# K^T by one crossbar transpose a head instead of 16 TensorE transposes, in a one-core attention forward and backward kernel

## Chip, cores and metric

The kernel runs on one core of a Trainium2 chip. The metric is the device time of one execution in microseconds (us); lower is better. Executions of one kernel differ by some 0.2 to 0.6%, so what matters here is timed in several rounds, in turn with the kernel before on the same chip.

## The reference

One layer, forward and backward, in bf16. S = 2048 rows, D = 576, H = 32 heads of 128, F = 4608:

```python
def _A_ref(x, k_cache, v_cache, wq, wo):
    q = (x @ wq).reshape(B, Sq, H, Dh).transpose(0, 2, 1, 3)
    scores = jnp.einsum("bhqd,bhkd->bhqk", q, k_cache) * (Dh ** -0.5)
    p = _softmax(scores, axis=-1)
    o = jnp.einsum("bhqk,bhkd->bhqd", p, v_cache)
    return o.transpose(0, 2, 1, 3).reshape(B, Sq, H * Dh) @ wo
# ... _B_ref: a gated MLP
xn = _layernorm(x);  s = _A_ref(xn, ...);  g = _silu(_B_ref(xn, ...))
return x + s * g
# the outputs: this, and its gradients by x, k_cache, v_cache, wq, wo, w_gate, w_up, w_down
```

## The kernel before

Each head takes two phases of 16 slots, one slot for each block of 128 query rows. In a slot of phase 1 TensorE (PE) makes 128 x 2048 scores from Q^T and K^T, ScalarE (ACT) makes their exponentials into a slab `Pq`, and the SP queue turns the slab with the DMA crossbar into `PT`, which PE reads five slots later (`skew` is 5). Phase 2 does the same for the gradients: `dp` on PE, `Pq` rewritten by ACT and VectorE (DVE), turned into `dST`, read five slots later. So 32 crossbar transposes of 512 KB a head run on one queue.

K is loaded as `Kn`, 16 blocks with keys on the partitions. The scores need K^T, in `KT`, half of the tile `KQ`. K^T of head h+1 is made in phase 2 of head h, because phase 1 of head h still reads `KT`:

```python
def prep_kt(hs):
    KTv = hs.KT[:].rearrange("p (t q) -> p t q", q=P)
    pe_transpose_blocks(lambda j: hs.Kn[:, j, :], 0, NT, lambda g, n: KTv[:, g:g + n, :], "s")

def transpose_slab(hs, qt, name):                      # PT and dST
    T = wpt.tile([P, NT, P], bf, name=name, tag="PT")
    nc.sync.dma_start_transpose(T[:], hs.slabs[qt][:])
    return T

def plan(h):
    # ...
    pl = b2 - 2 * NT if h else None                    # the first slot of phase 2 of head h - 1
    if h:
        for c in range(4):
            put(pl + q(c), 0, lambda c=c: load_k(hd(), c, 4))
            put(pl + q(skew + 3 + c), 0, lambda c=c: load_v(hd(), c, 4))
        # ...
        put(pl + q(skew + 3), NT * P, lambda: prep_kt(hd()))
    # ...
    for qt in range(NT):
        put(b2 + qt + skew, NT * P // 2, lambda qt=qt: tail2(hd(), qt, 0))   # reads dST of qt
        put(b2 + qt + skew, NT * P // 2, lambda qt=qt: tail2(hd(), qt, 1))
```

A scheduler orders each engine's instructions when the program is built, and may issue an instruction well before the slot in which the text has it. It moves the V loads, written in slots 8 to 11, to 9 to 15 us after the start of phase 2 (slots 3 and 4), and the K loads into phase 1.

## Time and profile before

| | before |
|---|---|
| time, first three runs | 5043.2 us (5036.47 to 5043.98) |
| attention, 32 heads | about 490 to 3650 us |
| one head, PE-bound: phase 1 + phase 2 | 49.56 + 48.13 us |

The page of the profile: busy time of an engine and its share of the span, then the share that the chain of waits gives each engine.

```profile
PE 4922.4 (97%) x53584; PEld 3474.9 (69%) x54480; DVE 2581.2 (51%) x6705; ACT 2574.1 (51%) x4636; POOL 950.4 (19%) x1481
...
PE 89%; issue 4%; DMA 3%; DVE 2%; ACT 1%; POOL 0%; SPq 0%; POOLq 0%; ACTq 0%; DVEq 0%
```

PE's own instructions are the limit. What the 16 transposes of a head cost there is read from the timeline of PE in head 4 (start, length, what). A group's length holds the latency of its last matmul, so cost is the distance between starts:

```profile
946.23 0.38 PE L698 MATMUL dp<-VT,dOT 128*128 128x512 bf16 x1
946.66 1.06 PE L146 MATMUL acct<-ident,Kn 128*128 128x128 bf16 x16
947.56 0.59 PE L698 MATMUL dp<-VT,dOT 128*128 128x512 bf16 x2
```

From 946.66 to 947.56 is 0.90 us: 56 ns a transpose. Two groups of the page's kind, the copies that leave PSUM and the reads of `dST` (after the first bar busy us and mean ns; after the second the engine's idle time before them and what ended it):

```profile
L40 ACT COPY KQ<-acct 128x1024 bf16<-128x1024 bf16 x62 | 59.7, 1015 | 15.8 <-PE acct L146 15.8
...
L675 PE MATMUL acc<-Kn,dST 128*128 128x128 bf16 x8192 | 551.3, 219 | 10.1 <-DMA dST<-Pq 6.5
```

The SP queue has two views that seem to disagree. Its waits in head 4 (870 to 972 us; us in total, times, longest):

```profile
SPq L622 <- ACT Pq L646: 32.8, 15, 4.7
SPq L622 <- DVE Pq L701: 15.2, 9, 3.7
SPq L622 <- DVE Pq L706: 14.4, 6, 3.4
SPq L622 <- DVE junk L687: 4.4, 2, 2.8
SPq L622 <- ACT o_n L48: 2.3, 1, 2.3
```

Together 69 us of 102. Its timeline from 900 to 972 us, in which neighbours are merged and the first group begins before the window:

```profile
894.76 31.29 SPq L622 DMA_TRANSPOSE PT<-Pq  x11
926.76 47.78 SPq L622 DMA_TRANSPOSE dST<-Pq  x16
```

### The profile page before, as it was taken

What the parts mean: (1) busy time and instruction counts of PE and PEld (TensorE: products, weight loads), DVE (VectorE), ACT (ScalarE), POOL (GpSimd) and SP (SyncE); (2) the same over time, 40 slices, a digit from 0 to 9 for tenths busy, and PEclk for the clock granted to TensorE, in tenths of its full rate; (3) what the DMA queues carried; (4) which work ended last, traced back from release to release, by engine and by line L of the source; (5) the groups of instructions that cost most, each with busy time, mean ns of one, the idle gap of its engine ahead of it and who ended that gap; (6) DMA issues with size and microseconds to landing.
All of it is one profiled execution on the core that took longest, in us unless ns stands there. A gap on an engine that the chain in (4) does not pass through costs nothing.

```text
span 5053.4 us, 128161 instructions
## 1 busy us (share of the span) xinstructions
PE 4922.4 (97%) x53584; PEld 3474.9 (69%) x54480; DVE 2581.2 (51%) x6705; ACT 2574.1 (51%) x4636; POOL 950.4 (19%) x1481
## 2 busy tenths in 40 slices
PE   8999999999999999999999999999789999999999
PEld 3445777777777787777778777777646666555554
DVE  4544666666566666666656666665425444200111
ACT  4432766666666676666667666666313333211000
POOL 3322111111111111111111111111122222211000
PEclk9999999999999999999999999999999999999999
DMA  7886999999999999999999999999996665797976
GB/s 249 271 202 171 212 208 211 203 211 209 207 214 214 201 212 207 210 205 211 214 202 209 215 206 207 208 213 202 197 201 204 193 183 181 213 266 187 173 141 121
DMA packets 2762675, 1031.39 MB, mean 204 GB/s; under 512 B 2665249, under 2 KB 2669474, under 8 KB 2762082
## 3 DMA queue, kind: packets, MB, share of 16 engines
q1 hardware_dynamic: 2659746, 699.38, 75.0%
q0 software_dynamic: 101728, 323.05, 20.1%
q8 instruction: 428, 7.01, 0.6%
q14 instruction: 165, 1.35, 0.1%
q10 hardware_dynamic: 608, 0.59, 0.0%
HBM read 175.31 MB, written 182.13 MB: 71 GB/s over the span
## 4 chain that ended last, share of the span: by engine, by line
PE 89%; issue 4%; DMA 3%; DVE 2%; ACT 1%; POOL 0%; SPq 0%; POOLq 0%; ACTq 0%; DVEq 0%
PE acc L734 17%; PE acc L675 17%; PE acc L960 13%; PE sp L628 7%; PE acc L1131 7%; PE dp L698 7%; PE acc L213 6%; PE g_ps L446 3%; PE u_ps L448 3%; PE dh L1013 3%; PE acc L531 2%; PE acct L146 2%; PE acc L930 2%; DMA dST<-Pq 1%; DVE Pq L701 1%
## 5 line engine op out<-in xcount | busy, mean ns | idle before, releaser
L646 ACT ACTIVATE Pq<-sp 128x1024 bf16<-128x1024 f32 x1024 | 1047.1, 1023 | 330.4 <-PE sp L628 199.1
L734 PEld LDWEIGHTS <-Pq 128*128 128x128 bf16 x16384 | 1002.9, 98 | 240.5 <-issue 1.1
L705 ACT ACTIVATE t<-dp,negdelta 128x1024 bf16<-128x1024 f32 x512 | 571.1, 1116 | 222.6 <-PE dp L698 169.0
L701 DVE SCALAR_TENSOR_TENSOR Pq<-dp,negdelta,Pq 128x1024 bf16<-128x1024 f32 x512 | 654.9, 1279 | 38.6 <-PE acc L675 37.5
L675 PEld LDWEIGHTS <-PT 128*128 128x128 bf16 x8192 | 503.3, 98 | 142.2 <-DMA PT<-Pq 20.9
L675 PE MATMUL acc<-Vn,PT 128*128 128x128 bf16 x8192 | 548.4, 219 | 26.6 <-DMA PT<-Pq 19.6
L675 PE MATMUL acc<-Kn,dST 128*128 128x128 bf16 x8192 | 551.3, 219 | 10.1 <-DMA dST<-Pq 6.5
L734 PE MATMUL acc<-dOn,Pq 128*128 128x128 bf16 x8192 | 547.4, 219 | 10.2 <-DVE junk L687 0.2
L628 PE MATMUL sp<-KQ 128*128 128x512 bf16 x1762 | 548.4, 380 | 2.6 <-ACT Pq L646 2.4
L698 PE MATMUL dp<-VT,dOT 128*128 128x512 bf16 x1728 | 540.0, 379 | 7.6 <-DVE Pq L701 7.6
L734 PE MATMUL acc<-Qn,Pq 128*128 128x128 bf16 x8192 | 540.6, 219 | 3.4
L706 DVE TENSOR_TENSOR Pq<-t,Pq 128x1024 bf16<-128x1024 bf16 x512 | 354.3, 692 | 365.8 <-ACT t L705 359.0
L675 PEld LDWEIGHTS <-dST 128*128 128x128 bf16 x8192 | 492.0, 98 | 69.5 <-DMA dST<-Pq 8.6
L715 ACT ACTIVATE dq_n<-acc,rsc 128x128 bf16<-128x128 f32 x512 | 188.1, 367 | 333.0 <-PE acc L675 331.9
L1147 DVE SCALAR_TENSOR_TENSOR junk<-acc,xn_all 128x512 f32<-128x512 f32 (+1 forms) x32 | 13.9, 453 | 637.0 <-ACT dxn L1146 637.0
L748 POOL DMA_DIRECT2D out_dram<-kvo x256 | 140.2, 548 | 1019.0 <-DVE kvo L746 1011.0
L669 POOL DMA_DIRECT2D on_d<-o_n x128 | 97.0, 758 | 750.7 <-DVE junk L687 396.7
L1015 DVE TENSOR_TENSOR du_blk<-dh,ah 128x256 bf16<-128x256 f32 x288 | 120.1, 417 | 191.6 <-PE dh L1013 189.5
L50 DVE TENSOR_SCALAR o_n<-acc,rinv_all 128x128 bf16<-128x128 f32 x352 | 123.2, 350 | 180.9 <-PE acc L675 180.9
L1146 ACT ACTIVATE dxn<-acc 128x512 f32<-128x512 f32 (+1 forms) x32 | 12.8, 406 | 393.6 <-PE acc L1131 386.2
L633 DVE TENSOR_REDUCE rs_all<-rsp 128x1 f32<-128x2 f32 x512 | 78.0, 152 | 256.3 <-ACT Pq L646 254.1
L646 ACT ACTIVATION_READ_ACCUMULATOR Pq<-sp 128x1 f32 x1024 | 200.4, 196 | 0.0
(206 smaller groups left out, 6949.9 us busy)
## 6 DMA issues: line engine op xcount, KB each, us to landing
out_dram<-kvo POOLq DMA_DIRECT2D x256, 128.0 KB, 4.2
ah<-a_d POOLq DMA_DIRECT2D x18, 1024.0 KB, 7.1
ah<-h_d POOLq DMA_DIRECT2D x18, 1024.0 KB, 9.5
du_d<-du_blk POOLq DMA_DIRECT2D x18, 1024.0 KB, 8.1
dg_d<-dg_blk POOLq DMA_DIRECT2D x18, 1024.0 KB, 9.9
h_d<-h_row POOLq DMA_DIRECT2D x64, 256.0 KB, 3.5
a_d<-a_row POOLq DMA_DIRECT2D x64, 256.0 KB, 3.7
x_all<-in_A_k_cache_dram SPq DMA_DIRECT2D x64, 256.0 KB, 4.0
```

What stands on the lines that cost most here:

```text
L213: nc.tensor.matmul(av[:, :CH], lhsT=w[:, i, :], rhs=srcT[:, i, cs], start=(i == 0), stop=(i == DT - 1))
L628: nc.tensor.matmul(sp[:, c * CH:(c + 1) * CH], lhsT=hs.QT[:, qt * P:(qt + 1) * P], rhs=hs.KT[:, hf * HW_ + c * CH: hf * HW_ + (c + 1) * CH ...
L646: nc.scalar.activation(Pq[:, hsl], sp[:], AF.Exp, scale=SCALE, accum_out=hs.rsp[:, hf:hf + 1])
L675: nc.tensor.matmul(hs.acc[:, 0, :], lhsT=T[:, kt, :], rhs=rhs[:, kt, :], start=(kt == 0), stop=(kt == NT - 1))
L698: nc.tensor.matmul(dp[:, c * CH:(c + 1) * CH], lhsT=hs.dOT[:, qt * P:(qt + 1) * P], rhs=hs.VT[:, hf * HW_ + c * CH: hf * HW_ + (c + 1) * C ...
L701: nc.vector.scalar_tensor_tensor(Pq[:, hsl], dp[:], hs.negdelta[:, qt:qt + 1], Pq[:, hsl], op0=ALU.add, op1=ALU.mult)
L705: nc.scalar.activation(t[:], dp[:], AF.Identity, bias=hs.negdelta[:, qt:qt + 1], scale=1.0)
L706: nc.vector.tensor_tensor(Pq[:, hsl], t[:], Pq[:, hsl], op=ALU.mult)
L715: nc.scalar.activation(hs.dq_n[:, qt % G4, :], hs.acc[:, 0, :], AF.Copy, scale=hs.rsc[:, qt:qt + 1])
L734: nc.tensor.matmul(self.tile[:, j, :], lhsT=self.slabs[qt][:, kt * P:(kt + 1) * P], rhs=self.rhs[:, qt, :], start=(qt == self.lo), stop=(q ...
L960: nc.tensor.matmul(accs[j][:, :nn], lhsT=lhs[:, st, cols], rhs=rhs[:, st, n0:n0 + nn], start=(st == 0), stop=(st == NT - 1))
L1131: nc.tensor.matmul(self.accs[sl][j][:, :nn], lhsT=ch[:, kk, sl * P:(sl + 1) * P], rhs=wT[:, k0 + kk, n0:n0 + nn], start=(self.k + kk == 0) ...
```

## The change

The intent is to take work from PE, the limit, and give it to the DMA crossbar, which does 32 such transposes a head already. K^T of head 0 is still made on PE, before attention.

```diff
+            def turn_nat(dst, src):
+                nc.sync.dma_start_transpose(dst[:].rearrange("p (t q) -> p t q", q=P), src[:].rearrange("p t d -> p (t d)"))
+
             def start_head(h):
...
-                    put(pl + q(skew + 3), NT * P, lambda: prep_kt(hd()))
+                    put(pl + q(skew + 3), 0, lambda: turn_nat(hd().KT, hd().Kn))
```

In the built program the scheduler does not leave the new transpose in slot 8. It puts it between the 15th and the 16th `PT` of the previous head, where its wait, for the last score matmul that reads `KT`, ends. The orders of ACT, DVE and POOL differ by ACT's removed copies alone, that of PE by the removed transposes and one `dp` pair a head moved within its slot.

## The prediction

> **What bounds the kernel.** The page gives PE 97% busy, the chain of waits 89% PE. Attention (486 to 3590 us, 32 heads, 97.0 us each) has PE busy 3040 of 3104 us in the stretch table, DVE 63%, ACT 68%. The timeline of a middle head (874 to 971 us) is back-to-back matmuls with one PE wait of 0.24 us. In all of attention the wait list gives PE 18.2 us for PT transposes (15.4 of it once, in the last head) and 2.3 us for dST. So PE instruction time is the limit; DMA, at 9 in the page's slices, is nearly hidden.
>
> **What changes.** Removed for 31 heads: 16 PE transposes and two ACT copies of 1.015 us. In the timeline the 16 transposes start at 946.66 and the next matmul at 947.56: 0.90 us, 56 ns each, like any 128-column matmul. (The Trainium skill, "TensorE: Matmul & The Clock Gate", Part 4, gives about 275 ns for one; here 219 ns is the latency, hidden by the pipeline. At 275 ns 4.4 us a head, 2.7%, would be saved; I do not believe it.) PE saves 31 x 0.89 = 27.6 us, 0.55%. The copies are off the path: PE never waits for them.
>
> Added: a 512 KB crossbar transpose a head on the SP queue, 33 instead of 32. The instruction order shows it between the previous head's 15th and 16th PT, waiting for PE (the last score matmul that reads K^T) and four Kn loads. POOL, DVE and ACT orders are otherwise unchanged; on PE one dp pair moves within its slot. Kn landed by about 900 us in that head, the scores end at 922, K^T is needed at 971: 40 us of slack, and no blocking on loads.
>
> **Cost of the addition.** SP waits for compute 69 of 97 us, so issuing has room. Transposes land in 3.6 to 3.9 us uncontended, in 8 to 9 beside the Kn and Vn loads, and recover 1 to 2 us per 2.65 us slot, so one occupies about 2 us (estimate; 512 KB at the 261 GB/s of the skill's "DMA: Bandwidth & Descriptors", "DMA_TRANSPOSE effective BW", is also 2.0). It delays the last PT and the first one or two dST by about 2 us, where landing is 3.7 to 5.5. A dST is issued at 926.76 and read at 937.82, so 11 us are there. Tight are the dST beside the Vn loads (landing 9.0, slack 2), 12 us later: the backlog should be gone. I allow 3 us in all for new waits.
>
> **Prediction.** 5043.2 - 27.6 + 3: about 5019 us (ratio 0.995), range 5008 to 5034. Faster by over 2%: 0.01; within 2%: 0.97; slower: 0.02.
>
> **What would show it.** The head period falls from 97.0 to 96.1 us, the difference all in attention. PE busy falls by about 27 us. The matmuls acct<-Kn fall from 496 to 0, the ACT copies KQ<-acct from 62 to 0. KQ<-Kn appears as 31 DMA transposes landing in 4 to 7 us. PE waits for PT and dST stay under 30 us. DMA bytes rise by 16 MB.
>
> **What would make it wrong.** The new transpose blocks its queue (Kn late in other heads, or its wait on PE is for a later instruction than the last score matmul): every PT and dST behind it is late, several us a head, over 100 us. Or DMA is nearer saturation than landing times suggest, and dST waits appear in each head. Or DVE, 94% busy early in the second phase, paces the shortened slot, so less than 0.89 us a head is won.

## More of the kernel before

PE waited for `dST` only 6.5 us in the whole run.

Last, how loaded the DMA engines are around the start of phase 2 in head 20 (at 2487.0 us), by stretch: length, busy time of PE, PEld, DVE, ACT and POOL (with counts), granted clock, DMA share, GB/s. The share adds up packet times over 16 engines and can pass 1, as it does here.

```profile
2479.00:2487.00 8.00, 7.90 (x113) 6.77 (x114) 4.63 (x23) 6.29 (x12) 0.00 (x0) 1.00 1.15 216
2487.00:2491.00 4.00, 3.71 (x50) 2.93 (x48) 3.52 (x11) 2.96 (x6) 0.75 (x1) 1.00 0.82 197
2491.00:2499.00 8.00, 7.89 (x107) 6.56 (x109) 6.84 (x13) 3.77 (x6) 0.88 (x2) 1.00 0.84 190
2499.00:2507.00 8.00, 7.89 (x110) 6.60 (x110) 7.12 (x10) 4.38 (x7) 3.67 (x7) 1.00 1.11 213
```

For the first 12 us of phase 2 the engines have less to do (0.82, 0.84); then the V loads come (POOL, last row) and they are full again. Head 20 shows this more strongly than most: as means over heads 1 to 30 the four stretches have 1.19, 1.13, 1.02 and 1.13, so what there is of quiet lies 4 to 12 us into the phase.

## The result, and the profile after

| | before | after |
|---|---|---|
| median of 4 runs | 5043.59 us (5036.47 to 5046.36) | 5046.65 us (5040.28 to 5060.24) |
| ratio, 95% interval | | 1.0012 (0.9987 to 1.0036) |

Ratios here are the mean time of one kernel's runs over the mean of the other's in the same rounds, so they are not quite the ratio of the medians that are quoted. About 5019 us was predicted; the time did not move. The page, then the transposes' tile, groups and PE waits:

```profile
PE 4900.6 (97%) x53089; PEld 3447.6 (68%) x53984; DVE 2585.6 (51%) x6705; ACT 2520.8 (50%) x4574; POOL 950.7 (19%) x1481
...
PE 86%; DMA 7%; issue 4%; DVE 2%; ACT 1%; POOL 0%; SPq 0%; POOLq 0%; ACTq 0%; DVEq 0%
```

```profile
L610 SPq DMA_TRANSPOSE KQ<-Kn x31: 1471/2627/3736, 534.4 to 3473.3; - x31
```

```profile
L678 PE MATMUL acc<-Kn,dST 128*128 128x128 bf16 x8192 | 557.1, 219 | 34.1 <-DMA dST<-Pq 28.9
```

The 496 weight loads (PEld) of the transposes are gone, 54480 to 53984, and DMA's share of the chain rose from 3% to 7%. (PE's busy time is not compared closely: 896 of its matmul records are missing before and 895 after, against the weight loads, and in e_sp10 and e_split none.) PE now waits 28.9 us for `dST` instead of 6.5. The lengths of the phases, taken from the starts of their first weight loads, say it most plainly. Before, phase 2 is 48.13 us in 27 of 31 heads. After, it is 47.24 us in the best heads, 0.89 us less, just as predicted; but in 17 of 31 it is longer by over 0.3 us, up to 51.88 us, and the 31 together exceed 31 x 47.24 by 35.6 us. Phase 1 is 49.56 us in nearly every head of both.

Head 4 has the 51.88 us. Its SP queue, 900 to 975 us:

```profile
899.93 24.04 SPq L625 DMA_TRANSPOSE PT<-Pq  x9
924.15 2.74 SPq L610 DMA_TRANSPOSE KQ<-Kn  x1
926.99 3.24 SPq L625 DMA_TRANSPOSE PT<-Pq  x1
930.31 44.99 SPq L625 DMA_TRANSPOSE dST<-Pq  x16
```

and the PE waits in its phase 2 (idle time and releaser in brackets):

```profile
941.01 1.07 PE L678 MATMUL acc<-Kn,dST 128*128 128x128 bf16 x16 [1.41 <-DMA dST<-Pq]
...
945.83 1.07 PE L678 MATMUL acc<-Kn,dST 128*128 128x128 bf16 x16 [1.55 <-DMA dST<-Pq]
...
951.60 1.07 PE L678 MATMUL acc<-Kn,dST 128*128 128x128 bf16 x16 [1.18 <-DMA dST<-Pq]
```

This phase starts at 921.78 us, 1.03 before that of the kernel before, yet its first `dST` is issued at 930.31 instead of 926.76. Issuing K^T took 2.74 us; the `PT` behind it was held back and, with its own issue slowed to 3.24 us, held back the first `dST`. The DMA engines, as before for head 20 (phase 2 from 2494.7 us):

```profile
2486.70:2494.70 8.00, 7.90 (x113) 6.70 (x114) 4.70 (x23) 6.29 (x13) 0.00 (x0) 1.00 1.20 216
2494.70:2498.70 4.00, 3.72 (x50) 2.95 (x49) 3.50 (x10) 2.96 (x6) 0.75 (x1) 1.00 1.19 268
2498.70:2506.70 8.00, 6.95 (x90) 5.53 (x91) 6.84 (x13) 3.77 (x7) 0.55 (x1) 1.00 1.16 186
2506.70:2514.70 8.00, 7.77 (x106) 6.53 (x109) 6.52 (x10) 3.43 (x6) 3.99 (x7) 1.00 1.16 264
```

The quiet 12 us are gone: 1.19 and 1.16 where it was 0.82 and 0.84. PE loses in the third row (6.95 of 8 us instead of 7.89). Over heads 1 to 30 the step is smaller and still there: in the third stretch 1.19 in the mean instead of 1.02.

The next table is worked out from every transpose's record in the traces, as means over heads 1 to 30. "Idle" is the SP queue's pause before a `dST` (its start less the end of the issue before); "slack" is the time from a `dST`'s landing to its first use on PE; a dash stands where the trace does not tell the landing, and in some kernels it tells it in part of the heads only (26 or 27 of 30 in after and e_novn, 14 to 16 in e_half and e_sp10).

| kernel | idle before dST 0, 1, 2, 3, 4 | slack of dST 0, 1, 2, 3, 4 |
|---|---|---|
| before | 1.32, 0.69, 0.78, 0.69, 0.11 | 6.3, -, 6.2, 2.1, 2.2 |
| after | 0.09, 0.10, 0.14, 0.16, 0.10 | 3.9, 3.9, 2.5, 0.9, 0.9 |
| e_none | 1.34, 0.63, 0.88, 0.70, 0.09 | 6.4, -, 6.1, 1.9, 1.2 |
| e_copy | 0.26, 0.21, 0.46, 0.40, 0.09 | -, -, 5.2, 1.5, 0.9 |
| e_novn | 0.10, 0.10, 0.11, 0.11, 0.10 | 3.9, 4.3, 3.9, 3.0, 3.2 |
| e_half | 0.45, 0.16, 0.52, 0.56, 0.11 | 5.4, 5.8, 5.2, 1.6, 1.1 |
| e_sp10 | 1.33, 0.43, 0.97, 0.71, 0.13 | 6.5, 6.5, 6.3, 2.4, 1.8 |

Before, the queue had 3.5 us of pause before dST 0 to 3 (1.32 + 0.69 + 0.78 + 0.69) and next to none before dST 4 to 10 (0.09 to 0.18); before dST 11 to 15 they are 0.4 to 1.1 us again. After, those in front are used up (0.49 us left): the first dST is issued 6.2 us after the start of phase 2 instead of 4.0, and dST 4 18.5 instead of 15.2. PE waited for dST 2 most (10.9 us) and for dST 3 (9.8). Of dST 4's lost slack the removal alone explains 1.0 us (e_none, 1.2 instead of 2.2). A single profile is not enough for more: the same kernel profiled again showed 13.4 us of such waits in its steady heads (486 to 3480 us) where the first showed 26.1. The time from the start of the last head to the end of the program is between 1515 and 1542 us in the profiled executions, with a mean granted clock between 0.984 and 0.992, though no edit touches that stretch but for an order of the SP queue told of below. So the rest is timed as well.

### The profile page after: what moved, and what is told of

The parts are those of the page before. It is cut to its first block, busy times and chain, and to the rows that moved or that the text cites. A ratio compares the mean times of both kernels' runs of the same rounds, so it can differ in the third digit from the quotient of the medians.

```text
span 5058.4 us, 127199 instructions
## 1 busy us (share of the span) xinstructions
PE 4900.6 (97%) x53089; PEld 3447.6 (68%) x53984; DVE 2585.6 (51%) x6705; ACT 2520.8 (50%) x4574; POOL 950.7 (19%) x1481
## 3 DMA queue, kind: packets, MB, share of 16 engines
q8 instruction: 424, 6.95, 0.6%
## 4 chain that ended last, share of the span: by engine, by line
PE 86%; DMA 7%; issue 4%; DVE 2%; ACT 1%; POOL 0%; SPq 0%; POOLq 0%; ACTq 0%; DVEq 0%
PE acc L737 17%; PE acc L678 16%; PE acc L963 13%; PE sp L631 7%; PE dp L701 6%; PE acc L1134 6%; PE acc L213 6%; DMA dST<-Pq 3%; PE g_ps L446 3%; PE u_ps L448 3%; PE dh L1016 3%; PE acc L531 3%; PE acct L146 2%; PE acc L933 1%; DMA KQ<-on_d 1%
## 5 line engine op out<-in xcount | busy, mean ns | idle before, releaser
L678 PE MATMUL acc<-Kn,dST 128*128 128x128 bf16 x8192 | 557.1, 219 | 34.1 <-DMA dST<-Pq 28.9
```

The lines of the kernel that those rows point to most:

```text
L678: nc.tensor.matmul(hs.acc[:, 0, :], lhsT=T[:, kt, :], rhs=rhs[:, kt, :], start=(kt == 0), stop=(kt == NT - 1))
```

## The experiments

My first theory, T1 in the expectations: the new transpose takes 2.6 us of the transposing queue where the queue has no time to spare, so the dST behind it come late to the place where the V loads slow their landing. Rivals: total DMA load, wherever it stands (T2), or the loss of the 0.9 us by which the PE transposes had put off the use of dST (T3). In six of the ten programs every order but the one named is that of the changed kernel. In the other four (e_sp12, e_sp8, e_sp10, e_split) the SP queue is kept in the order of the text, and this moves two more transposes, once in the program: those of the stage behind attention, `xnT` and `KQ` from `on_d`. The scheduler had put them among the last head's PT, as SP's timeline of e_again shows:

```profile
3542.15 4.84 SPq L582 DMA_TRANSPOSE xnT<-on_d  x1
3547.08 15.85 SPq L625 DMA_TRANSPOSE PT<-Pq  x6
3563.02 5.25 SPq L582 DMA_TRANSPOSE KQ<-on_d  x1
```

In the four they stand behind the last head's dST, as SP's timeline of e_sp10 shows:

```profile
3563.42 43.89 SPq L625 DMA_TRANSPOSE dST<-Pq  x16
3607.42 4.68 SPq L582 DMA_TRANSPOSE KQ<-on_d  x1
3612.15 6.41 SPq L582 DMA_TRANSPOSE xnT<-on_d  x1
```

No run keeps the SP queue so with K^T at its first place, so the times of the four do not show what K^T's place alone is worth. From the start of the last head to the first `dh` matmul, which follows the stage behind attention, their profiled executions take 267 us in the mean (256 to 276), the eight others 277 (262 to 284): some 10 us, 0.2%, may come from there (an estimate; the ranges overlap, so it may also be chance). The last column below is free of it: it is what the 31 second phases before the last head exceed 47.24 us by, together, and in how many heads by over 0.1 us (e_extra: over 48.13, since its PE transposes remain). In the first profile of the changed kernel this is 35.6 (17), in the kernel before, over 48.13, 3.4 (4).

"PE waits" below are those of the profiled execution from 486 to 3480 us; waits for PT and K^T are given where they exceed 2 us.

| run | median us (before, same chip) | ratio (95% interval) | PE waits for dST, us | second phases over, us (heads) |
|---|---|---|---|---|
| e_none | 5020.2 (5048.0) | 0.9937 (0.9917 to 0.9958) | 1.3 | 1.9 (4) |
| e_sp12 | 5022.0 (5048.0) | 0.9953 (0.9931 to 0.9975) | 4.2, and 7.2 for K^T | 20.1 (15) |
| e_sp8 | 5025.4 (5048.0) | 0.9946 (0.9927 to 0.9965) | 11.9, and 2.5 for PT | 15.4 (10) |
| e_extra | 5059.5 (5048.0) | 1.0020 (1.0000 to 1.0040) | 14.8 | 20.2 (10) |
| e_again | 5041.0 (5046.1) | 0.9986 (0.9970 to 1.0002) | 13.4 | 17.2 (15) |
| e_copy | 5046.5 (5046.1) | 0.9999 (0.9981 to 1.0018) | 9.2, and 3.7 for PT | 17.1 (12) |
| e_novn | 5023.4 (5046.1) | 0.9953 (0.9937 to 0.9968) | 0.8 | 1.5 (3) |
| e_half | 5036.3 (5046.1) | 0.9972 (0.9951 to 0.9993) | 9.0 | 11.7 (11) |
| e_sp10 | 5020.4 (5042.8) | 0.9952 (0.9937 to 0.9966) | 3.7 | 4.9 (5) |
| e_split | 5020.3 (5042.8) | 0.9953 (0.9939 to 0.9966) | 3.1 | 4.4 (5) |

### The removal alone (e_none)

```diff
-                    put(pl + q(skew + 3), 0, lambda: turn_nat(hd().KT, hd().Kn))
```

> The change with its DMA transpose left out too (K^T stays that of head 0, so results are wrong on purpose): the removal alone; every other engine's order as in the changed kernel. T1 (the transpose takes 2.6 us of a transposing queue that has no idle time where it stands): second phases at 47.2 us in nearly every head, ratio to before 0.995 (about 5016 us). T2 (total DMA load, place does not matter): the same 0.995. T3 (the PE transposes gave the dST transposes 0.9 us of slack, and the waits come from losing that): second phases still above 47.2 in many heads, ratio 0.998 to 1.000.

The ratio is 0.9937, and phase 2 is 47.2 us in 27 of 31 heads. From the groups of PE:

```profile
L678 PE MATMUL acc<-Kn,dST 128*128 128x128 bf16 x8192 | 556.4, 219 | 7.8 <-DMA dST<-Pq 2.8
```

So the removal is worth what was predicted (0.63% of 5048 us is 32 us, interval 21 to 42; 27.6 predicted), and T3 as the whole cause is out: without the added transfer the waits stay away. (T1 and T2 both expected this, so the run does not part them.) One warning: K^T here is that of head 0 in every head, and the outputs still pass the comparison with the reference, as they do in e_copy and e_half below, where K^T is wrong too. That comparison therefore cannot tell whether a kernel makes K^T right.

### The same transpose, later in the queue (e_sp12, e_sp8)

e_sp12; e_sp8 has the second of its two edits alone:

```diff
-                    put(pl + q(skew + 3), 0, lambda: turn_nat(hd().KT, hd().Kn))
+                    put(pl + q(12), 0, lambda: turn_nat(hd().KT, hd().Kn))
...
-        attention(True)
+        with tc.manual_schedule(engines={mybir.EngineType.SP}):
+            attention(True)
```

Moving the line to slot 12 alone does nothing: in a program built so, and not run, the scheduler hoists the transpose to the same place. Keeping the SP queue in the order of the text puts it behind dST 12, or dST 8.

> The changed kernel with the SP queue kept in program order and the K^T transpose behind dST 12 of the previous head, where the queue of before had 0.8 to 1.1 us idle per transpose and dST 8 to 11 us of slack; nothing else moves on any engine. T1: ratio 0.995 to 0.996 (5016 to 5022 us), PE waits for dST under 10 us. T2: as the changed kernel, ratio 0.999 to 1.003. T3: 0.998 to 1.002.

> The same with the K^T transpose behind dST 8, where the program text has it: the queue has no idle time there (0.09 us between issues) but the dST that follow have 5 to 11 us of slack. T1 (what counts is the slack of the transposes behind it): ratio 0.995 to 0.997. A rival form of T1 (what counts is idle time of the queue at that place): 0.999 to 1.002. T2: 0.999 to 1.003.

Both are faster than before (0.9953 and 0.9946), with the same transposes and the same bytes, as T1 expected. But their profiles do not show that K^T's place did it: the second phases are over by 20.1 and 15.4 us, about as much as e_again's 17.2, and e_sp12's profiled execution gains on e_again's in the last head and behind it (1515 us instead of 1537), where the two moved transposes stand. (e_sp8's profiled execution is the slowest of its five.) So these two runs alone do not decide between T1 and T2; e_sp10 and e_split, below, tell more. What they do show is what each place costs: behind dST 12 PE waits 8 times for K^T at the start of the next head; behind dST 8 the slack of dST 9 to 11 falls to between 3.2 and 3.9 us. The queue is on time again for the first dST in both (issued 4.1 and 4.0 us into phase 2), and what PE waits for is dST 3 and 4, which stand in front of the moved transpose.

### The addition alone (e_extra)

```diff
                     put(pl + q(skew + 3), 0, lambda: turn_nat(hd().KT, hd().Kn))
+                    put(pl + q(skew + 3), NT * P, lambda: prep_kt(hd()))
```

> The changed kernel with the 16 PE transposes and their copies kept as well (both write the same K^T): the addition alone, results right. T1: the dST waits appear in the second phase without any saving; but the PE transposes still give 0.9 us of slack, so the cost is 10 to 36 us, ratio 1.002 to 1.007. T2: about 28 to 36 us, 1.006 to 1.007. T3 (the addition is harmless, the lost slack does it): ratio 0.999 to 1.001.

The ratio of 1.0020 is about 10 us (0.0020 x 5048), at the low end of the range; its interval reaches down to none (1.0000), so by time alone T3's range is not excluded here. The second phases are over by 20.2 us instead of 3.4 in the kernel before. With the PE transposes removed the addition costs more by time: e_again less e_none is 0.0049, 25 us, and the first measurement less e_none 0.0075, 38 us. That is the direction in which T3's 0.9 us of slack would work, as an amplifier (dST 4 keeps 2.2 us of slack in e_extra, 0.9 in the changed kernel); but the second phases of e_again are over by no more than e_extra's, so whether it amplifies stays open.

### The changed kernel again (e_again)

> The changed kernel itself, unedited, for its time on the same chip as the three others. Ratio to before 0.999 to 1.004, dST waits of 20 to 40 us in the second phases.

The file was not edited. The ratio of 0.9986 touches the lower edge of what was expected, and the waits (13.4 us) are below it. Over both measurements (1.0012 and 0.9986) the change lies between a loss of 0.4% and a gain of 0.3%.

### The same bytes by another queue (e_copy)

```diff
-                    put(pl + q(skew + 3), 0, lambda: turn_nat(hd().KT, hd().Kn))
+                    put(pl + q(skew + 3), 0, lambda: nc.gpsimd.dma_start(hd().KT, hd().Kn[:].rearrange("p t d -> p (t d)")))
```

> The transpose replaced by a plain copy of the same 512 KB into K^T's place (wrong on purpose), issued from POOL with the same waits and at the same time, so the bytes stay and the SP queue is as in before; SP, PE, ACT and DVE orders do not move. If what costs is the place in the transposing queue (T1): ratio 0.994 to 0.996, with dST issued 4.0 us into the second phase as in before. If it is traffic on the DMA engines at that moment: 0.999 to 1.002, with dST landing later after an unchanged issue.

0.9999: the ratio falls on the other branch, and T1 in the form that I had given it falls. The SP queue holds 32 transposes again, and neither the time nor the second phases (over by 17.1 us) are better than in e_again. The granted clock was lower in these six runs (0.9947 in the mean, before 0.9964), which may account for some 0.2% of the time (an estimate), but not for the second phases, where it was 0.999 and more. The stretches of e_copy's head 20 (phase 2 from 2480.7 us) show a traffic peak where before was quiet (third row, 1.26 instead of 0.84; in the mean over heads 1 to 30, 1.18 instead of 1.02):

```profile
2472.70:2480.70 8.00, 7.89 (x113) 6.70 (x114) 4.70 (x23) 6.30 (x13) 0.35 (x1) 1.00 1.31 263
2480.70:2484.70 4.00, 3.72 (x50) 2.95 (x49) 3.51 (x10) 2.96 (x6) 0.95 (x2) 1.00 0.89 260
2484.70:2492.70 8.00, 7.88 (x107) 6.56 (x109) 6.85 (x13) 3.77 (x7) 0.80 (x2) 1.00 1.26 231
2492.70:2500.70 8.00, 7.90 (x111) 6.58 (x111) 7.12 (x10) 4.39 (x7) 3.75 (x7) 1.00 1.09 183
```

In the means over heads, the issue of the 16th PT takes 3.62 us instead of e_none's 1.94, though nothing was added to its queue, and the pauses of the queue before dST 0 to 3 fall from 3.55 to 1.33 us. So traffic of another queue lengthens an issue on this one, and the new bytes cost at that moment though they stand in no place of the SP queue. That the place in the queue adds nothing is not shown: the first dST is issued 4.6 us into phase 2 here, before 4.0, in the changed kernel 6.2 and in e_again 5.9, and PE waits here mostly for dST 4, there for dST 2 and 3. (The branch had expected an unchanged issue; it was not unchanged.) That different queues share the engines is what the Trainium skill says in "DMA: Bandwidth & Descriptors", section "Issuing engines are not separate DMA queues": DMAs that different engines start run on the same 16 DMA engines and interleave.

### Without the V loads (e_novn)

```diff
-                        put(pl + q(skew + 3 + c), 0, lambda c=c: load_v(hd(), c, 4))
```

> The changed kernel without the V loads of heads 1 to 31 (V stays that of head 0, wrong on purpose); only POOL loses instructions. T1 says that the dST issued beside the V loads, 9 to 15 us into the second phase, are the ones that run out of slack because the queue comes late to a place where landing takes 8 to 9 us: without V loads those waits vanish although the K^T transpose stays where it is, ratio 0.994 to 0.996. If the late queue is enough by itself: dST waits over 15 us, ratio 0.998 or more.

0.9953, and the dST waits vanish; from the list of PE waits:

```profile
PE acc L678 <- DMA dST<-Pq: 0.8, 2, 0.4
```

The queue is as late as in the changed kernel (idle 0.10, first slack 3.9 us), but dST 3 and 4 keep 3.0 and 3.2 us instead of 0.9. Both are needed: a queue that comes late out of the quiet stretch, and the V loads behind it. (The run also leaves out as many bytes as the K^T transposes add, so by itself it does not speak against T2.) The result is wrong; the comparison reports a relative error of 1.40.

### Half the transpose (e_half)

```diff
+                    put(pl + q(skew + 3), 0, lambda: turn_nat(hd().KT[:, :NT * P // 2], hd().Kn[:, :NT // 2, :]))
```

(in place of the full one; half of K^T is stale)

> The K^T transpose moves only 8 of the 16 blocks (wrong on purpose), at the same place. If its cost goes with the time it holds the queue (2.6 us for 16 blocks, I expect 1.3 to 1.7 us for 8): ratio 0.995 to 0.998, dST waits about a third of those of the changed kernel. If any transpose at that place costs the same: 0.999 to 1.003.

Its issue took 1.41 us in the mean, and the ratio of 0.9972 lies between e_none (0.9937) and e_again (0.9986), as a cost that goes with size should. The dST waits of 9.0 us are more than the third that was expected, if e_again's 13.4 is the measure.

### A better place (e_sp10, e_split)

e_sp10 is e_sp12 with slot 10. e_split is this, with the SP queue kept in the order of the text too:

```diff
+                    put(pl + q(9), 0, lambda: turn_nat(hd().KT[:, :S // 2], hd().Kn[:, :NT // 2, :]))
+                    put(pl + q(11), 0, lambda: turn_nat(hd().KT[:, S // 2:], hd().Kn[:, NT // 2:, :]))
```

> As the run behind dST 12, but behind dST 10: behind dST 8 the dST 9 to 11 had only 3.2 to 3.9 us of slack left, behind dST 12 the next head waited 8 times for K^T (7.2 us). If the place in time is what counts (the traffic must miss the dST 1 to 4 and still land before the next head): ratio 0.9935 to 0.9955, dST and K^T waits of PE together under 10 us. If the load of 33 transposes costs something wherever it stands: no better than the two others, 0.995 to 0.997.

> The K^T transpose as two of 8 blocks, behind dST 9 and dST 11 (1.4 us of queue each in the half-size run). If short pieces spread over the queue's small gaps hold up the others less: at or below the run behind dST 10, ratio 0.993 to 0.995. If a second issue costs about what it saves: the same within 0.1%.

Both give 5020 us, 0.9952 and 0.9953: faster than the kernel before, lower in ratio than the changed one (1.0012, 0.9986), and not to be told apart from no transfer at all (e_none, 0.9937; their intervals overlap). Some 0.2% of this may be the two moved transposes at the end of attention. e_sp10's ratio lies in both of the ranges that were expected, so the ratio does not decide between them. In e_sp10, SP's timeline of head 4 and the reads of dST over the whole run:

```profile
897.27 26.80 SPq L625 DMA_TRANSPOSE PT<-Pq  x10
924.29 32.68 SPq L625 DMA_TRANSPOSE dST<-Pq  x11
957.14 1.81 SPq L610 DMA_TRANSPOSE KQ<-Kn  x1
959.04 13.74 SPq L625 DMA_TRANSPOSE dST<-Pq  x5
```

```profile
L678 PE MATMUL acc<-Kn,dST 128*128 128x128 bf16 x8192 | 556.4, 219 | 4.3 <-DMA dST<-Pq 4.3
```

The first dST are issued on time again, and the 31 second phases exceed 47.24 us by 4.9 us together, in e_split by 4.4, against 35.6 and 17.2 in the two profiles of the changed kernel; 5 heads are hit in each, there 17 and 15. In those heads the SP order differs by K^T's place alone, and the bytes are the same; 4 to 12 us into phase 2 the DMA share of e_sp10 is 1.01 in the mean over heads 1 to 30, as in e_none (1.01), against 1.19 in the changed kernel. This is what speaks against T2: the place counts. It is the evidence of one profile each, and why e_sp12 and e_sp8, at neighbouring places, are not as good in theirs stays open. Splitting gains nothing over e_sp10, and the late places cannot be told apart by their ratios.

## Why the prediction was wrong

- **The limit is PE, and the removal saves 27.6 us: right.** Phase 2 fell by 0.89 us wherever nothing interfered (48.13 to 47.24), and e_none gained 0.63%, with 27.6 us (0.55%) inside its interval. The prediction was also right to take 56 ns a transpose from the timeline and not the 275 ns that the Trainium skill gives ("TensorE: Matmul & The Clock Gate", Part 4), which would have promised 2.7%.
- **Where the transpose goes in the queue and what it waits for: right; what it delays: too few.** No wait for a load blocks the queue, and "the last PT and the first one or two dST" are late by about 2 us, in head 4 by more. But the delay does not end there: dST 4 is issued 3.3 us later in its phase than before.
- **"The backlog should be gone", and "I allow 3 us in all for new waits": wrong.** This is the failed term of the sum. By time the addition costs about 25 us (e_again less e_none) to 38 us (the first measurement less e_none), nearly all of the saving or all of it; by the second phases of the two profiles 15 to 34 us (17.2 and 35.6, less e_none's 1.9). The forecast allowed 3. The lateness was not made up before the V loads, 12 us later: dST 3 and 4 kept 0.9 us of slack in the mean instead of 2.1 and 2.2 (with the removal alone 1.9 and 1.2), so in about half of the heads PE stood still.
- **Why I thought so: "SP waits for compute 69 of 97 us, so issuing has room": wrong.** That number counts the queue's issuing as waiting. From starts and ends, SP was idle 22% of heads 1 to 29 (628 of 2836 us, some 22 us a head), and nearly half of that lies at the start of phase 1 (9.6 us a head); before dST 0 to 3 there were 3.5 us, and the new transpose took 2.6 us and lengthened the issue of the PT behind it from 1.91 to 2.87 us. "One occupies about 2 us" was near the truth (2.6 us of issue; the other transposes of the changed kernel take 2.3 us in the median, half of them between 1.8 and 3.1). What failed was the room, not the cost.
- **"DMA is nearer saturation than landing times suggest", listed under what would make it wrong: this is what happened,** though in some heads and not in each. DVE pacing the short slot, and a blocked queue, did not.
- **My own theory after the result was half right.** That the place matters held, by the second phases of e_sp10 and e_split; by their times, and e_sp12's and e_sp8's, it is not cleanly shown, since the two transposes at the end of attention moved too. That the place *in the queue* is all that matters fell to e_copy: traffic at that moment is enough. How much each of the two adds is not shown.
- **Open:** which heads are hit, why the same kernel's waits were 26.1 us in one profile and 13.4 in another, and what keeping the SP queue in the order of the text is worth by itself. Whether K^T comes out right is not shown by the comparison, which passes with a stale K^T; it rests on the transpose's access pattern being that of the PE blocks, read from the code.

## What to carry to other kernels

Before moving work from a busy PE to "idle" DMA, look for the moment at which it will run: in this kernel the stretch from 4 to 12 us into phase 2 had a mean DMA share of 1.02, the stretches around it 1.13, and the kernels in which it was filled to 1.18 or 1.19 lost the gain. Count a queue's idle time from starts and ends, not from its wait list. If a scheduler hoists a transfer that is not urgent to the first moment its operands allow, pin it where the transfers behind it have slack to give, and read from the built program what else the pin moves: here the pinned programs turned no gain into one of 0.5%, of which some 0.2% may come from what else it moved.

## What the Trainium skill lacked or had wrong

- "TensorE: Matmul & The Clock Gate", Part 4, gives the duration of a 128 x 128 PE transpose, about 275 ns in a kernel, and no rate in a stream (the page's Part 1 has one, for plain matmuls). In a dense matmul stream the runs show 56 ns each (16 in 0.90 us); 219 ns is the duration of one. Who prices their removal in a PE-bound kernel by Part 4's figure overstates it five times.
- "DMA: Bandwidth & Descriptors", section "Issuing engines are not separate DMA queues", says that starting DMAs elsewhere only saves sequencer time. e_copy agrees (ratio 0.9999). The section does not say that another queue's traffic can lengthen the *issue* on a queue to which nothing was added: 1.94 to 3.62 us for the same transpose (e_none, e_copy).
- "VectorE: DVE Perf Modes", section "Rules for kernel authors", advises TensorE for a 128 x 128 transpose if a PSUM destination is acceptable, the crossbar otherwise. Here PSUM was acceptable, and the better path depended on the moment: the crossbar gave ratios of 1.0012 and 0.9986 at one place and 0.9952 at another (with two later transposes moved as well). No page has this.
- "DMA: Bandwidth & Descriptors", table row "DMA_TRANSPOSE effective BW", gives 261 GB/s with a non-contiguous middle dimension, by which 512 KB would take 2.0 us (an estimate). No run times a transpose alone: beside other traffic the issues took 2.3 us in the median, and landing took 4.9 to 5.2 us in the medians of the kernel before. So the figure is neither confirmed nor contradicted.
